# Two layers of sliding-window attention and an MLP on one core: the order of attention turns and dense matmuls decided by a program-side clock, score maxima over 320 columns instead of 384, and staging of MLP weights in value buffers

## The chip, the core and the metric

The kernel runs on one core of a Trainium2 chip. The metric is the time of one execution on the device in microseconds (us); the runs shown of the kernel before have a median of 1614.45 us. Five engines work side by side, each with its own in-order queue: TensorE (PE, with its weight loads as PEld), VectorE (DVE), ScalarE (ACT), GpSimd (POOL) and SyncE (SP, which here only issues DMAs; ACT issues some too). Matmuls write to PSUM; the other engines move results from there to SBUF.

## What is computed

The input is 2048 rows of 640 values. The same pair of layers is applied twice: `x = x + attention(layernorm(x))`, then `x = x + mlp(layernorm(x))`.

```python
def _A_ref(x, wqkv, wo):                      # 32 heads of 20 values, window 256
    q, k, v = ...                             # x @ wqkv, cut into heads
    scores = jnp.einsum("bhqd,bhkd->bhqk", q, k) * (Dh ** -0.5)
    mask = (idx[:, None] - idx[None, :] >= 0) & (idx[:, None] - idx[None, :] < W)
    p = _softmax(jnp.where(mask[None, None], scores, -1e9), axis=-1)
    return heads_joined(p @ v) @ wo
def _B_ref(x, w1, b1, w2, b2):                # 640 -> 1536 -> 640
    h = x @ w1 + b1
    return jnp.where(h > 0, h, 0) ** 2 @ w2 + b2
```

## The kernel before, in words

**Tiling.** The 2048 rows are cut into 8 groups of 256 rows, and with the two layer pairs there are 16 units, numbered u = 0 to 15. Every fp32 operand of a dense matmul is split into a high and a low fp16 part, and three products (high-high, high-low, low-high) are summed; `mm3` (line 261) issues them in steps of about 500 ns. Dense work of a unit: the projections to queries and keys (`stage_qk`, QK below), to values (`stage_v`, V), the output projection (`stage_o`, O), and the two MLP matmuls (`stage_f`, F1 and F2). A dense accumulator is one of two PSUM banks of the pool "mm"; `mm_tile` takes the next free one. The attention output of a pass (`pv`) uses the same pool.

**Attention turns.** The 32 heads of a unit are worked off in 8 quads of four heads. A quad has three turns on PE. The max turn (`max_quad`, MX below, matmuls of lines 570 and 579) computes the scores of four head-and-row blocks into the six PSUM banks `bb`, and eight DVE instructions (line 592) add the mask and take the row maximum. The maxima of two quads are transposed (line 605) and written as extra rows of the queries by DMA. The exp turn (`exp_quad`, EX, lines 647 and 655) computes the transposed scores, with the maxima already subtracted, into the same six banks; six ACT instructions (line 669) take the exponential into `pt`, and POOL cuts the window's edges out (lines 684, 688). The value turn (`pv_quad`, PV, line 718) multiplies by the values. MX runs three quads ahead of EX (`LEAD`). Since MX and EX share the banks `bb`, an MX cannot start before ACT has read the last EX out, and an EX not before DVE has reduced the last MX.

From u = 2 on (`quarters`), MX and EX of a unit that is not the first of a layer cut each matmul into 64-row, 64-column tiles of the array, so that four run side by side and only the 320 of 384 columns that a 64-row half can see are computed. DVE still reads 384 columns. In MX the fourth block does not fit behind the others and is laid across the three banks, 128 columns in each.

**The order of the work** is made by the program itself when it is built. `now[0]` is a running estimate of PE's time, `clk` of the other engines', and `post` puts an instruction of another engine into a list that `pump` empties in order of priority when the estimate allows. `need` moves the estimate forward until a job's estimated end; PE's instruction stream is then written down with whatever comes next, so on the chip PE waits there if the estimate was too early. `flow` orders unit 0. For u = 1 to 15 `together` takes dense steps from a generator and puts in the attention turns when a share of the unit's dense cost is used up (`done < cost * share * part / total`), without asking whether the turn's inputs have come. Dense work that lies beside unit u is V and QK of u+1, O and the MLP of u-1. In u = 14 and 15 there is less of it, and `CARRY`, `KEEP` and `MID` move some from one to the next.

**Places that the change touches.** `load_o` (line 762) fetches a unit's attention output `od` from DRAM and normalizes it: per quarter a reciprocal (line 794), a product (797), a high part on ACT (801) and a low part (804). `stage_o` begins, for u = 0 alone, with `spin(40)`: 40 matmuls of a constant identity (line 275, 80 instructions in the trace, since fp32 takes two passes each), whose result nobody reads. `load_w2` brings the twelve row blocks of the second MLP weight through three thirds of the key buffer `kt2`, which has to be set to a constant (`set_row`) before keys of unit 2 come into it.

## Time and profile before

| | |
|---|---|
| median of 3 runs | 1614.45 us (1614.18 to 1614.67) |
| the profiled execution's own time | 1611.7 us |
| its span, first to last instruction | 1609.9 us |
| busy share: PE, PEld, DVE, ACT, POOL | 98%, 73%, 65%, 46%, 38% |
| granted TensorE clock, mean | 1.00 |

The span is cut below into the stretches between the last PV of one unit and the last PV of the next. "Idle" of PE in a stretch is its length minus PE's busy time. In rows of a timeline the first number is the start in us from the span's start, the second the duration of the merged group; a bracket at the end has the idle time of that engine just ahead of it and what ended it. Since matmuls are pipelined and a matmul's recorded end lies some 0.1 to 0.2 us behind the start of the next, PE times are taken from start to start where possible.

### The profile page before, as it was taken

To read this page: it belongs to the slowest core of one execution; us is meant where nothing else is said; L and a number is where in the kernel's file an instruction comes from. 1 tells how busy PE (TensorE), PEld (TensorE's weight loads), DVE (VectorE), ACT (ScalarE), POOL (GpSimd) and SP (SyncE) were. 2 spreads that over 40 slices of the span, in tenths; PEclk is the share of its full clock that TensorE was granted. 3 is DMA by queue.
4 is the path that set the end of the run, shared out by engine and by line. 5 is a ranking of instruction groups with operands and counts; after the bars stand their busy time and mean duration, and the time that the engine had idled before them with its cause. 6 is when DMAs were issued, how large, how long until landed. Compare 5 with 4: busy or idle time off the path is not lost.

```text
span 1609.9 us, 51896 instructions
## 1 busy us (share of the span) xinstructions
PE 1573.4 (98%) x21222; PEld 1178.3 (73%) x21222; DVE 1044.4 (65%) x3250; ACT 734.3 (46%) x1593; POOL 610.9 (38%) x1288
## 2 busy tenths in 40 slices
PE   8998999999999999999999999999999999998999
PEld 7676767777777777777777777777777777775667
DVE  8786865666757657665556766567675666757441
ACT  4554535344453444545343453534545444453522
POOL 1224434235353443535223352533534334353512
PEclk9999999999999999999999999999999999999999
DMA  9763243352434424343352534334343352431020
GB/s 270 206 169 103 60 121 80 99 127 50 120 84 111 97 67 119 74 121 80 95 133 54 122 80 124 81 95 111 66 115 86 107 109 52 111 73 55 27 65 18
DMA packets 234246, 158.56 MB, mean 98 GB/s; under 512 B 82200, under 2 KB 217752, under 8 KB 234008
## 3 DMA queue, kind: packets, MB, share of 16 engines
q1 hardware_dynamic: 227640, 145.74, 37.2%
q10 hardware_dynamic: 6368, 9.50, 2.0%
q8 instruction: 167, 2.74, 0.8%
q14 instruction: 71, 0.58, 0.1%
HBM read 84.68 MB, written 52.95 MB: 85 GB/s over the span
## 4 chain that ended last, share of the span: by engine, by line
PE 90%; DVE 4%; ACT 3%; issue 1%; DMA 1%; POOL 1%; SPq 0%; DVEq 0%; POOLq 0%; ACTq 0%
PE acc L261 67%; PE pv L718 10%; PE bb L647 4%; PE bb L570 4%; DVE bb L592 2%; ACT pt L669 1%; PE spin L275 1%; PE tr L605 1%; PE bb L655 1%; PE bb L579 1%; DMA od<-o 0%; ACT r L889 0%; DVE mx L592 0%; POOL pt L688 0%; DVE mT L610 0%
## 5 line engine op out<-in xcount | busy, mean ns | idle before, releaser
L592 DVE CUSTOM_DVE_ANT_0 bb<-bb,maskb 128x384 f32<-128x384 f32 (+2 forms) x1024 | 510.6, 566 | 101.0 <-PE bb L570 76.1
L669 ACT ACTIVATE pt<-bb 128x512 f32<-128x512 f32 (+1 forms) x736 | 375.8, 601 | 231.2 <-PE bb L647 199.5
L684 POOL TENSOR_SCALAR_AFFINE_SELECT pt<-pt 128x256 f32<-128x256 f32 x448 | 196.9, 445 | 556.2 <-ACT pt L669 534.3
L261 PE MATMUL acc<-y,w_s 128*128 128x256 f16 x2880 | 330.4, 273 | 4.5 <-DVE y L311 1.5
L261 PE MATMUL acc<-w_s,hh 128*128 128x320 f16 x2304 | 326.2, 299 | 0.0
L261 PEld LDWEIGHTS <-w_s 128*128 128x128 f16 x2880 | 277.4, 98 | 57.2 <-issue 23.5
L261 PEld LDWEIGHTS <-hh 128*128 128x128 f16 x2304 | 221.6, 98 | 96.9 <-issue 12.5
L261 PEld LDWEIGHTS <-wq_s 128*128 128x128 f16 x2400 | 230.6, 98 | 45.7 <-issue 15.2
L261 PE MATMUL acc<-yT,wq_s 128*128 128x256 f16 x2250 | 258.9, 273 | 3.6 <-ACT ot L730 1.6
L688 POOL TENSOR_SCALAR_AFFINE_SELECT pt<-pt 128x256 f32<-128x256 f32 x512 | 218.9, 450 | 94.0 <-ACT pt L669 93.1
L899 DVE TENSOR_TENSOR hh<-r,hh 128x256 f16<-128x256 f32 x192 | 92.6, 505 | 201.3 <-ACT hh L896 195.0
L718 PE MATMUL pv<-pt,vt 128*32 128x128 f32 (+1 forms) x3840 | 186.7, 329 | 2.7 <-DVE x L828 1.7
L893 POOL TENSOR_TENSOR r<-r 128x256 f32<-128x256 f32 x192 | 113.5, 612 | 179.0 <-ACT r L889 177.6
L730 ACT COPY ot<-pv 128x256 f32<-128x256 f32 x128 | 47.6, 372 | 276.6 <-PE pv L718 276.5
L592 DVE DVE_READ_ACCUMULATOR2_ANT mx<- 128x1 f32 x1024 | 144.4, 141 | 0.0
L261 PE MATMUL acc<-wo_s,od 128*128 128x320 f16 x960 | 138.7, 300 | 2.1 <-ACT od L801 1.3
L261 PE MATMUL acc<-wq_s,yT 128*128 128x320 f16 x900 | 132.2, 299 | 3.6 <-DVE y L311 1.9
L718 PEld LDWEIGHTS pv<-pt,vt 128*32 128x32 f32 x3840 | 103.5, 109 | 44.0 <-POOL pt L688 5.7
L889 ACT ACTIVATE r<-acc,b1s 128x256 f32<-128x256 f32 x192 | 80.5, 471 | 98.6 <-PE acc L261 95.8
L261 PEld LDWEIGHTS <-od 128*128 128x128 f16 x960 | 91.4, 98 | 44.7 <-issue 6.0
L261 PEld LDWEIGHTS <-yT 128*128 128x128 f16 x900 | 86.6, 98 | 41.1 <-issue 10.5
L298 POOL TENSOR_TENSOR bmv<-bmv,neghalf 128x1 f32<-128x1 f32 x64 | 43.8, 691 | 138.7 <-DVE bmv L292 137.9
(86 smaller groups left out, 1229.0 us busy)
## 6 DMA issues: line engine op xcount, KB each, us to landing
qt<-qk SPq DMA_DIRECT2D x30, 480.0 KB
kt<-qk SPq DMA_DIRECT2D x30, 480.0 KB
qk<-qd SPq DMA_DIRECT2D x17, 640.0 KB
o<-ot SPq DMA_DIRECT2D x256, 42.0 KB
od<-o SPq DMA_DIRECT2D x14, 640.0 KB
qk<-yl SPq DMA_DIRECT2D x13, 640.0 KB
qk<-qd SPq DMA_DIRECT2D x17, 320.0 KB
xt<-in_A_x_dram SPq DMA_DIRECT2D x16, 320.0 KB
```

Of the source, the lines that this page charges most:

```text
L261: nc.tensor.matmul(acc, lhs(a, c), rhs(b, c), start=(k == 0), stop=(k == 3 * nk - 1))
L570: nc.tensor.matmul(to, qt[r, p, i * P + 64 * h:i * P + 64 * (h + 1)], kt[r, p, a:b], start=True, stop=True, tile_position=(64 * e, 64 * h))
L592: nc.vector.tensor_tensor_reduce(out=v, in0=v, in1=mask, scale=1.0, scalar=-3.0e38, op0=ALU.add, op1=ALU.max, accum_out=accum),
L647: nc.tensor.matmul(bb[e][rows, k, o + a:o + b], kt[r, 2 * qd + j, ko + 64 * h:ko + 64 * (h + 1)], qt[r, 2 * qd + j, q0 * P + a:q0 * P + b] ...
L669: nc.scalar.activation(box["pt"][:, :o], bb[e][:, k, :o], AF.Exp, scale=SCALE / (QS * QS))
L684: nc.gpsimd.affine_select(out=m, in_=m, pattern=[[0, 2], [-1, P]], compare_op=ALU.is_gt, fill=0.0, base=0, channel_multiplier=1)
L688: nc.gpsimd.affine_select(out=m, in_=m, pattern=[[0, 2], [1, P]], compare_op=ALU.is_ge, fill=0.0, base=0, channel_multiplier=-1)
L718: nc.tensor.matmul(pv[32 * jj:32 * (jj + 1), q0 * P:(q0 + qn) * P], vf[:, c:c + 32], pj[:, j, :], start=(k == 0), stop=(k == len(steps) - ...
L730: nc.scalar.copy(ot[:, qd % 2], pv)
L889: nc.scalar.activation(box["r"], acc[:, f, :], AF.Relu, bias=b1s[:, f0 + f:f0 + f + 1], scale=1.0 / (YS * WS))
L893: nc.gpsimd.tensor_tensor(box["r"], box["r"], box["r"], op=ALU.mult)
L899: nc.vector.tensor_sub(hh[:, 1, f, :], box["r"], hh[:, 0, f, :])
```

## The change

1. **MX in packed blocks.** For units that are not the first of a layer each of the four blocks takes 320 columns, one behind the other, over bank borders (0, 320, 640, 960), and a DVE instruction covers 320 columns with a mask `maskq` that is shifted by 64 columns for the upper 64 rows. A piece that would cross a bank border is cut there, so a turn has 38 matmuls instead of 36. For the first unit of a layer the blocks are unbroken (8 matmuls instead of 10), and the mask is `maskw`. Masks are made with one more select and two copies on POOL at the start.
2. **`quarters` holds for u = 1 too**, except its first EX.
3. **Dense work and turns by the program's clock.** Dense generators yield a `Want` (the jobs whose end they need, and whether they need a free accumulator bank) ahead of each place where they would wait. A `Stream` stops there while the estimate says that it isn't due. In `together`, a turn is put in when its share of dense work is done and its own inputs have come by the estimate; if the stream is stopped and the turn's inputs are there, the turn goes first; if neither can go, the estimate moves to the first that can.
4. **No `spin(40)`** ahead of `stage_o(0)`.
5. **`load_w2` has five places** instead of three: two value buffers (`vt4`, `vt5`) and the thirds of `kt2`. The value buffers' constant columns (`set_sums`) are written when their last weight block has gone, and V of unit 2 waits for that. In `load_o` the work of u = 0 has priority 1 instead of 2.

```diff
+    def when(w):
+        if any(j.end is None for j in w.jobs):
+            return None
+        t = max([0.0] + [j.end for j in w.jobs])
+        if w.bank and len(banks2) > 1:
+            free = [max(j.end for j in b) + LAT for b in banks2 if b and all(j.end is not None for j in b)]
+            if not free:
+                return None
+            t = max(t, min(free))
+        return t
...
+        def go(self):
+            while not self.over:
+                if self.want is not None:
+                    t = when(self.want)
+                    if t is None or t > now[0]:
+                        return None
+                    self.want = None
+                c = next(self.gen, "over")
...
-        for c in range(FC):
+        used_by = {}
+        for c, place in enumerate((3, 4, 0, 1, 2, 3, 4, 0, 1, 2, 0, 1)):
...
-            st = krow[2][:, D * (c % 3):D * (c % 3 + 1)]
+            st = vts[1 + place][1][:, :D] if place > 2 else krow[2][:, D * place:D * (place + 1)]
...
-        return u % NG != 0 and u > 1
+        return u % NG != 0
...
+        if quarters(u):
+            flat = [b.rearrange("p a n -> p (a n)") for b in bb]
+            pieces = []
+            for w in range(4):
+                j, i = divmod(w, 2)
+                p, at = 2 * qd + j, 5 * Q * w
+                cuts = sorted({0, 5 * Q, *(z - at for z in (512, 1024) if 0 < z - at < 5 * Q)})
+                for o0, o1 in zip(cuts, cuts[1:]):
                     for h in range(2):
...
+                    reduce(e, w, flat[e][:, 5 * Q * w:5 * Q * (w + 1)], maskq, 5 * Q)
...
+        whole = not quarters(u) or n == NQ
...
-            if u == 0 and i == 0:
-                spin(40)
+            yield Want(*js[2 * i:2 * i + 2])
             need(*js[2 * i:2 * i + 2])
...
+        def work(part, w):
+            nonlocal done
+            while True:
+                t = when(w) if w else None
+                ready = t is not None and t <= now[0]
+                if done >= cost * share * part / total and (ready or not w):
+                    return
+                c = s.go()
+                if c is not None:
+                    done += c
+                elif ready or (s.over and not w):
+                    return
+                else:
+                    wait_any(*([w] if w else []), *([s.want] if s.want else []))
...
-            while done < cost * share * part / total:
-                c = next(dense, None)
-                if c is None:
-                    break
-                step(c)
-                done += c
```

**What moves on the engines.** Between unit 2 and unit 13 PE's dense steps and turns stand in the same order as before; only the pieces within an MX differ. Three places are different and matter below.

PE around O of unit 0 (`spin` is the constant identity, `od` the attention output, `pv` a PV turn; a `bb<-qt,kt` row is of an EX and a `bb<-kt,qt` row of an MX). Before:

```order
L655 MATMUL bb_126<-qt,kt_78 128x256
L275 MATMUL spin<-ident 128x128 x40
L261 LDWEIGHTS od
L261 MATMUL acc<-wo_s,od 128x320
...
L579 LDWEIGHTS qt
```

With the change:

```order
L736 MATMUL bb_130<-qt,kt_86 128x256
L327 LDWEIGHTS wq_s
L327 MATMUL acc<-yT,wq_s 128x256
...
L649 MATMUL bb_130<-kt_86,qt 64x192
L799 MATMUL pv<-pt,vt_89 32x256 x4
L799 MATMUL pv<-pt,vt_88 32x128 x4
L799 MATMUL pv<-pt,vt_91 32x128 x4
L799 MATMUL pv<-pt,vt_90 32x256 x4
L327 LDWEIGHTS od
L327 MATMUL acc<-wo_s,od 128x320
```

Ten QK matmuls, one MX and one PV now stand between the first EX of unit 1 and O, where the constants stood; O's thirty matmuls of its first two accumulators come behind them.

ACT at the start of unit 2 (`qd` is an evicted QK accumulator, `ot` an evicted PV, and line 801, then 882, the high part of the first quarter of O's operand). Before:

```order
L669 ACTIVATE pt<-bb_126 128x512
L435 ACTIVATE qd<-acc 128x2x256
L801 CAST od<-od 128x5x64
L730 COPY ot<-pv 128x256
L435 ACTIVATE qd<-acc 128x2x256
L435 ACTIVATE qd<-acc 128x256
```

With the change:

```order
L750 ACTIVATE pt<-bb_130 128x512
L506 ACTIVATE qd<-acc 128x2x256
L811 COPY ot<-pv 128x256
L506 ACTIVATE qd<-acc 128x2x256
L506 ACTIVATE qd<-acc 128x256
L882 CAST od<-od 128x5x64
```

The CAST has gone from ahead of three evictions that free PSUM banks to behind them.

PE in unit 15, around the second pair of O's accumulators (named by their numbers: before, 25940 and 26022 are the second pair; with the change 26337 is the first of it). Before:

```order
L261 MATMUL acc_25900<-wo_s_103,od_25539 128x320
L261 LDWEIGHTS od_25539
L261 MATMUL acc_25940<-wo_s_103,od_25539 128x320
...
L570 MATMUL bb0_125<-kt2_79,qt_23909 64x128
...
L718 MATMUL pv_25985<-pt_25895,vt5_95 32x256
...
L261 MATMUL acc_26022<-wo_s_103,od_25539 128x320
```

With the change:

```order
L327 MATMUL acc_26270<-wo_s_107,od_25949 128x320
L728 LDWEIGHTS qt_24298
L728 MATMUL bb0_129<-qt_24298,kt2_87 64x192
...
L327 MATMUL acc_26337<-wo_s_107,od_25949 128x320
...
L649 MATMUL bb0_129<-kt2_87,qt_24298 64x256
```

Before, four matmuls of 25940 stood ahead of an MX; now a whole EX stands between the first pair of O's accumulators and the second.

More of the change, by code (lines that the diff above doesn't have):

```diff
@@ L17 @@
 P = 128
+Q = P // 2
 S = 2048
@@ L641, in exp_quad @@
                 for j in range(2):
-                    for h in range(2 if quarters(u) else 0):
+                    for h in range(0 if whole else 2):
                         a, b = (0, w - 64 * (1 - h)) if kb < 2 else (64 * h, w)
@@ L944, in run @@
     def run(*gs):
-        for c in chain(*gs):
-            step(c)
+        s = Stream(chain(*gs))
+        while not s.over:
+            if s.go() is None and not s.over:
+                wait_any(s.want)
     SHARE = 0.55
@@ L1005, in together @@
                 late.clear()
+        work(part, None)
         if whole:
-            run(dense)
+            while not s.over:
+                if s.go() is None and not s.over:
+                    wait_any(s.want)
     QKC, VC, OC, FCST, LNC, CARRY, KEEP, MID = 16.4e3, 8.2e3, 8.2e3, 39.2e3, 1.2e3, 15e3, 20e3, 8e3
```

184 lines of the change are left out of this document (121 added, 63 removed).

## The prediction

> **What bounds the kernel now.** I read the page first, then busy time by stretch, then the waits of PE in the stretches where it is idle.
>
> ```profile
> span 1609.9 us, 51896 instructions
> PE 1573.4 (98%) x21222; PEld 1178.3 (73%) x21222; DVE 1044.4 (65%) x3250; ACT 734.3 (46%) x1593; POOL 610.9 (38%) x1288
> ```
>
> PE is busy 1573.4 of 1609.9 us, so it is idle for 36.5 us, and no other engine comes near it. What can be won is PE's idle time and whatever PE does in vain. The busy time by stretch (length, then PE, PEld, DVE, ACT and POOL busy, clock, DMA share, GB/s) says where the idle time lies; the stretches are unit 0, 1, 2, 3, then 14, 15 and the end.
>
> ```profile
> 0.00:105.60 105.60, 95.66 (x939) 72.82 (x939) 84.13 (x284) 55.16 (x111) 19.41 (x46) 1.00 0.80 218
> 105.60:204.80 99.20, 94.93 (x1139) 70.49 (x1135) 74.19 (x215) 49.02 (x105) 41.96 (x84) 1.00 0.38 98
> 204.80:304.30 99.50, 96.55 (x1394) 72.22 (x1390) 64.08 (x199) 45.14 (x98) 38.77 (x84) 1.00 0.40 98
> 304.30:401.50 97.20, 97.06 (x1402) 72.89 (x1398) 64.46 (x199) 45.37 (x98) 39.51 (x84) 1.00 0.39 95
> 1364.40:1452.40 88.00, 84.84 (x1299) 63.99 (x1296) 57.60 (x182) 43.90 (x96) 39.07 (x82) 1.00 0.35 87
> 1452.40:1534.50 82.10, 73.13 (x1066) 50.35 (x1063) 45.84 (x144) 37.76 (x84) 36.48 (x80) 1.00 0.13 40
> 1534.50:1610.00 75.50, 70.14 (x556) 54.12 (x553) 23.21 (x52) 15.13 (x37) 13.31 (x20) 1.00 0.14 44
> ```
>
> Idle per stretch is 9.9, 4.3, 3.0, 0.1, 3.2, 9.0 and 5.4 us, together 34.9 of the 36.5. Units 3 to 13 leave nothing. So the change is priced at its two ends: units 0 to 2, and units 14 and 15.
>
> **Unit 1: the constants go.** PE around O of unit 0:
>
> ```profile
> 109.52 1.19 PE L655 MATMUL bb<-qt,kt 62*128 62x256 f16 x16
> 110.64 9.20 PE L275 MATMUL spin<-ident 128*128 128x128 f32 x80
> 119.67 4.24 PE L261 MATMUL acc<-wo_s,od 128*128 128x320 f16 x30
> 123.84 0.84 PE L579 MATMUL bb<-kt,qt 60*128 60x128 f16 x18
> 126.35 1.51 PE L718 MATMUL pv<-pt,vt 128*32 128x256 f32 x32 [1.67 <-DVE x L828]
> 127.79 3.30 PE L261 MATMUL acc<-wo_s,od 128*128 128x320 f16 x23
> 136.07 0.84 PE L579 MATMUL bb<-kt,qt 60*128 60x128 f16 x18
> 136.83 1.51 PE L718 MATMUL pv<-pt,vt 128*32 128x256 f32 x32
> 141.73 1.79 PE L261 MATMUL acc<-wq_s,yT 128*128 128x320 f16 x12 [1.37 <-DVE y L311]
> 146.29 2.20 PE L261 MATMUL acc<-wq_s,yT 128*128 128x320 f16 x15 [0.52 <-DVE y L311]
> ```
>
> From the EX at 109.52 to the O rows behind the PV, at 127.79, pass 18.27 us. In them are 80 constant matmuls, 119.67 - 110.64 = 9.03 us, that compute nothing, and a PV that waits 1.67 us. That time isn't simply free: O needs its operand `od`, and DVE has it ready in this order:
>
> ```profile
> 113.60 0.96 DVE L794 RECIPROCAL rs<-rs 128x64 f32<-128x64 f32 x2
> 115.49 0.89 DVE L797 TENSOR_TENSOR od<-od,rs 128x320 f32<-128x320 f32 x2 [0.93 <-DMA od<-o]
> 116.76 0.82 DVE L804 TENSOR_TENSOR od<-od 128x320 f16<-128x320 f32 x2
> ```
>
> The load lands at 115.49, and the second low part, with which O may start, ends at 117.58. With the change ten QK matmuls (0.11 us each, by the row at 219.31 below; 1.1 us) come behind the EX, so the EX starts at about 108.4. The MX must wait for the six exponentials, then PV follows, then O. DVE's order is also another one: from the load's landing it does one product, two reciprocals, a low part, two products, a reciprocal and then the second low part, by the rows above 2 x 0.45 + 0.45 + 3 x 0.48 + 2 x 0.41 = 3.6 us. So `od` is ready at 119.1, or about 118 if the load lands 1.1 us earlier, as the PV ahead of it does. O's thirty matmuls (4.17 us) then end at 122.2 to 123.3, with MX and PV already done. Against 127.79 that is 4.5 to 5.6 us; I take **5.0**. If the load were to land 1 us later it would be 3.6; if it were there at once, the six exponentials, MX (0.7) and PV (1.4) would still hold O. The last four exponentials of that EX are this row:
>
> ```profile
> 111.67 2.08 ACT L669 ACTIVATE pt<-bb 128x512 f32<-128x512 f32 x4
> ```
>
> They end at 113.75, 4.2 us behind the EX's start, so O could not begin before 108.4 + 4.2 + 2.1 = 114.7, which would give 8.9. These are the ends.
>
> What follows in unit 1: MX 136.07 to 136.83 takes 0.76 us with 18 whole matmuls. In the tiled form it takes 0.68, by these rows of unit 2:
>
> ```profile
> 214.33 0.76 PE L570 MATMUL bb<-kt,qt 60*64 60x128 f16 x36
> 215.01 1.51 PE L718 MATMUL pv<-pt,vt 128*32 128x256 f32 x32
> 219.31 1.80 PE L261 MATMUL acc<-yT,wq_s 128*128 128x256 f16 x15 [1.59 <-ACT ot L730]
> 222.20 1.25 PE L261 MATMUL acc<-wq_s,yT 128*128 128x320 f16 x8 [1.10 <-DVE qd L438]
> ```
>
> Eight MX and seven EX become tiled, 15 x 0.08 = **1.2 us**. The waits of 1.37 and 0.52 us behind the transposes of the MLP's input are for an accumulator bank; behind the first of them now stands an EX (0.7 us) that needs none: **0.7** (0 to 1.9).
>
> **Unit 2: an operand that is late no longer blocks evictions.** The two waits in the last rows, 2.7 us, come from one load:
>
> ```profile
> 218.00 0.49 DVE L797 TENSOR_TENSOR od<-od,rs 128x320 f32<-128x320 f32 x1 [1.33 <-DMA od<-o]
> 218.53 0.46 ACT L801 CAST od<-od 128x320 f16<-128x320 f32 x1 [5.63 <-DVE od L797]
> ```
>
> ACT stood 5.63 us at the CAST of `od`, with the evictions of PV and QK queued behind it, and PE waited for those banks. In the changed order the CAST stands behind these evictions on ACT, and DVE does its MX reductions ahead of the product. Both waits should go: **2.7**; if the product is late for the low parts on DVE still, 1.1 of it stays.
>
> **Units 3 to 13: nothing.** PE's order is the same, and an MX has 38 pieces instead of 36. An EX with 32 pieces has the recorded length of an MX with 36:
>
> ```profile
> 1518.82 0.75 PE L647 MATMUL bb<-qt,kt 62*64 62x192 f16 x32
> ```
>
> That is 0.75 against 0.76 us for the same 1280 columns on each of the four tiles, so it is columns and not pieces that count, and I take 0. In proportion to pieces it would be 0.68 x 2/36 = 0.04 us a turn, 4 us in the 112 turns; columns are unchanged, so a gain is excluded. DVE's reductions get shorter:
>
> ```profile
> L592 DVE CUSTOM_DVE_ANT_0 bb<-bb,maskb 128x384 f32<-128x384 f32 x896 | 469.3, 591 | 87.7 <-PE bb L570 76.1 <-PE bb L579 9.1 <-ACT pt L669 1.8
> L592 DVE CUSTOM_DVE_ANT_0 bb<-bb,maskb 128x256 f32<-128x256 f32 x64 | 27.2, 463 | 0.0
> ```
>
> 128 columns are worth 591 - 463 = 128 ns, so 64 are worth 64 ns, 0.51 us over the eight of a turn, 57 us in all 112 turns. In these units it lies beside a PE that is idle for 0.1 us a stretch, and is worth nothing. That a block now spans a bank border shows in no row; DVE reading it slower by as much as a whole turn's 0.5 us would only undo this gain.
>
> **Units 14 and 15.** PE's waits from 1364.4 to 1534.5 (total, times, longest):
>
> ```profile
> PE bb L570 <- ACT pt L669: 3.4, 8, 1.0
> PE bb L647 <- DVE mx L592: 3.4, 9, 1.1
> PE acc L261 <- ACT od L801: 1.3, 1, 1.3
> PE acc L261 <- DVE y L311: 0.9, 1, 0.9
> PE acc L261 <- DVE od L804: 0.8, 1, 0.8
> ```
>
> With little dense work between the turns, MX waits for ACT to empty the banks and EX for DVE. The EX waits: nine, averaging 0.38 us, each turn's worth up to 0.51 less; all but the longest should go, 2.4. The two waits for `od` (2.1) should go, since an EX now stands ahead of the second half of O. Of the MX waits (3.4) and those behind the transposes (0.9, and some smaller ones) I give about half, 2.5, to turns that are put in when the estimate has their banks free; in units 14 and 15 seven of the thirteen distances from an EX to the MX behind it hold more PE work than before, three the same and three less. In all **7 us** (2 to 12, the last being all of the idle 12.2).
>
> **Parts at nothing.** The extra mask work on POOL falls into the first 6 us, where POOL is idle for 3.4 us ahead of line 298:
>
> ```profile
> 5.85 0.55 POOL L298 TENSOR_TENSOR bmv<-bmv,neghalf 128x1 f32<-128x1 f32 x1 [3.44 <-DVE bmv L292]
> ```
>
> One select and two copies, each at most as long as the first two selects by their smaller size, need about 1.5; without that cover the first layernorm would move by as much. The w2 blocks are as many as before, converted by the same instructions and loaded by as many DMAs from ACT's queue; five instead of three are converted ahead of O of unit 0, in a stretch where DVE is busy for 84.1 of 105.6 us, and V of unit 2 now waits for two of them, behind O, where the cover is the rest of unit 1. SP's and POOL's queues get no other instruction.
>
> **Sum.** 5.0 + 1.2 + 0.7 + 2.7 + 7.0 = 16.6 us. The profiled execution took 1611.7 us, 1.8 more than its span, so it should come to 1595.1; the median of the runs, 2.75 above that execution, to **1597.9**.
>
> **Rivals.**
>
> *The array goes cold.* In the new order PE has nothing between the end of PV (108.4 + 4.2 + 0.7 + 1.4 = 114.7) and O at 118 to 119.1: 3.3 to 4.4 us without a matmul. The constants stood exactly there. The trace shows what a rested array does: the first 24 constants of the program took 5.5 us, 0.229 each, against 9.03/80 = 0.113 ahead of O.
>
> ```profile
> L275 PE MATMUL spin<-ident 128*128 128x128 f32 x24 | 5.5, 428 | 1.4 <-POOL ident masks.py:199 1.4
> ```
>
> If that comes back, as many matmuls of O run at half speed: 24 x 0.116 = 2.8 us, giving 1600.7. The granted clock in the rows is 1.00 in every stretch and so doesn't show this state at the start. The Trainium skill, page "TensorE: Matmul & The Clock Gate", section "Part 1: The HAM clock gate", speaks against this part of the change: after an idle window of some 3.4 us, which runs free of the program, the array falls to half its clock, and about as long a busy one brings it back. By that rule a wait as long as this one would sometimes contain a whole window and mostly not; at the program's start the trace agrees. Chance 0.2.
>
> *The tail's waits only move.* The program's estimate, not the chip, says when banks are free; three of the thirteen EX-to-MX distances shrink, one to 2.8 us of PE work (an EX and fifteen matmuls of O, 0.68 + 15 x 0.139) where six exponentials take over 4. If what DVE gives is lost there, the 7 becomes 0: 1604.9. For it: the waits for ACT are as large as those for DVE. Against it: the shrunken ones lie beside O, where ACT evicts nothing else. Chance 0.13.
>
> *Slower: the weight loads of the extra pieces come to light.* A piece of 64 columns streams faster than its weights are loaded (recorded length 107 ns), and the new order has three such pieces in a row on the two tiles of the lower rows, where the old one had no three:
>
> ```profile
> L570 PEld LDWEIGHTS <-qt 60*64 60x64 f16 x3744 | 60.0, 107 | 29.1 <-issue 29.0
> ```
>
> If each of the two extra loads showed in full, a turn would be 0.21 longer, 24 us in 112 turns: 1597.9 + 24 = 1621.9. It decides from 16.6/112 = 0.15 us a turn. Against it: 32 and 36 pieces take the same time today. Chance 0.05.
>
> *The load is there early and the tail gives all:* 5.0 becomes 8.9 and 7 becomes 12: 1589.0. Chance 0.07.
>
> *The change doesn't do what it says:* between units 3 and 13 it doesn't, since PE's order is the same there; that is in the forecast.
>
> **How the numbers follow.** The forecast, 1597.9, has the remaining 0.55. The range leaves out the slower rival and the outermost parts of the others: from 1589.0 (all of the early load and the tail) to 1606.0 (tail lost, with 1 us of the pieces). About 0.2% (3.2 us) is what a measurement of this kernel can tell from no change. Faster by more than that, below 1611.2, are the forecast, the cold array, the moved waits and the early load but for a few per cent where several meet: 0.91; slower, above 1617.7, is the rival with the weight loads: 0.05; same: 0.04.
>
> **What would show it.** No constants behind the first EX of unit 1, and PE idle for 3 to 5 us ahead of O; matmuls of O spaced 139 ns (twice that if cold). The waits at 219.31 and 222.20 gone. Stretches of units 3 to 13 at 97.2 us still, and MX to PV 0.68. Reductions of 320 columns near 527 ns. PE idle in units 14 and 15 at about 5 us instead of 12.2. It would be wrong if units 3 to 13 change in length, if O starts later than before, or if the EX-to-MX waits grow.

## The result, and the profile after

The changed kernel took **1593.83 us** (median of 4 runs, 1593.23 to 1598.94) beside 1614.32 us of the kernel before (4 runs, 1613.78 to 1614.67). The ratio is 0.9879, 95% interval 0.9866 to 0.9893. The forecast was 1597.9 with a range of 1589.0 to 1606.0.

The profiled execution is the slowest of the four, 1598.94 us. A second profile of the same kernel, taken for the experiment `a_again` below (1595.61 us), stands beside it, since the two differ in what matters. Below is the length of each stretch, taken on PE from the matmul behind the last PV of one unit to that of the next (before: 1611.7 us).

| stretch | before | forecast | first profile | second profile |
|---|---|---|---|---|
| units 0 to 2 | 302.92 | -9.6 | 297.40 (-5.5) | 295.15 (-7.8) |
| units 3 to 13 | 1060.09 | 0 | 1062.99 (+2.9) | 1062.83 (+2.7) |
| units 14 and 15 | 170.08 | -7.0 | 159.92 (-10.2) | 159.03 (-11.1) |
| end | 72.14 | 0 | 72.17 | 72.16 |
| all | 1605.23 | -16.6 | 1592.48 (-12.8) | 1589.17 (-16.1) |

From one profiled execution to the other 12.8 or 16.1 us were gained, and 20.5 between the medians: the profile of before was 2.6 us quicker than its median, the first of after 5.1 us slower than its own.

The first lines of the page after the change, and the row of the shortened reductions:

```profile
span 1597.2 us, 52634 instructions
PE 1564.5 (98%) x21590; PEld 1171.1 (73%) x21590; DVE 981.5 (61%) x3251; ACT 735.1 (46%) x1593; POOL 611.3 (38%) x1291
```

```profile
L629 DVE CUSTOM_DVE_ANT_0 bb<-bb,maskq 128x320 f32<-128x320 f32 x896 | 409.0, 522 | 94.9 <-PE bb L649 79.1 <-ACT pt L750 7.3 <-ACT r L974 5.8
```

A reduction takes 522 instead of 591 ns, as forecast (527), and DVE is busy for 63 us less. PE's busy time fell by 8.9 us: 9.03 of constants went. Its idle time fell by only 3.8 us (32.7 instead of 36.5): units 14 and 15 gave 8.8, but unit 1 has 2.3 more than before (6.6 instead of 4.3, from new waits) and units 3 to 13 together 2.8 more. Part of the busy time is now matmuls at half clock, which take longer. Busy time by stretch of the same profile (length, then PE, PEld, DVE, ACT and POOL busy, the granted clock, DMA share, GB/s), for units 1, 2, 3, 14, 15 and the end:

```profile
105.60:200.30 94.70, 88.10 (x1284) 63.45 (x1284) 68.96 (x222) 48.10 (x104) 42.84 (x84) 0.98 0.40 98
200.30:298.80 98.50, 96.23 (x1410) 72.13 (x1406) 59.66 (x199) 45.39 (x98) 39.13 (x84) 1.00 0.42 98
298.80:396.20 97.40, 97.07 (x1418) 72.92 (x1414) 60.10 (x199) 45.40 (x98) 39.11 (x84) 1.00 0.41 95
1361.80:1446.40 84.60, 84.46 (x1323) 63.91 (x1320) 53.33 (x186) 43.84 (x96) 38.56 (x82) 1.00 0.39 90
1446.40:1521.70 75.30, 72.03 (x1082) 51.31 (x1079) 41.63 (x142) 38.99 (x86) 37.94 (x82) 0.98 0.16 48
1521.70:1597.20 75.50, 70.21 (x542) 53.48 (x538) 23.27 (x52) 14.21 (x35) 12.59 (x19) 0.98 0.13 40
```

Two things are to be seen. PE is idle in units 14 and 15 for 0.14 + 3.27 = 3.4 us instead of 12.2. And the clock is 0.98 in three stretches that had 1.00 before. Where the clock fell first shows PE's timeline around O of unit 0 (start, duration; in brackets the idle time ahead and what ended it):

```profile
109.49 0.83 PE L736 MATMUL bb<-qt,kt 62*128 62x256 f16 x16
110.26 1.27 PE L327 MATMUL acc<-yT,wq_s 128*128 128x256 f16 x10
113.46 0.27 PE L649 MATMUL bb<-kt,qt 60*64 60x256 f16 x1 [1.94 <-ACT pt L750]
113.95 0.75 PE L649 MATMUL bb<-kt,qt 60*64 60x256 f16 x37 [0.22 <-ACT pt L750]
114.64 1.87 PE L799 MATMUL pv<-pt,vt 128*32 128x256 f32 x32
118.79 0.45 PE L327 MATMUL acc<-wo_s,od 128*128 128x320 f16 x2 [2.29 <-ACT od L882]
119.51 5.65 PE L327 MATMUL acc<-wo_s,od 128*128 128x320 f16 x28 [0.28 <-DVE od L885]
```

The constants are gone; MX and PV stand in their place. MX waits 1.94 us for the six exponentials, and O behind PV waits another 2.29 us for `od`. Then 28 matmuls of O take 5.65 us, where thirty took 4.24. The same stretch of the second profile, cut along the pieces of 3.41 us in which the trace records the clock (PE's busy time is the second number, the clock the third from the right):

```profile
109.28:112.69 3.41, 1.67 (x24) 1.18 (x19) 3.41 (x6) 2.79 (x6) 2.19 (x3) 1.00 0.85 193
112.69:116.11 3.42, 2.82 (x70) 1.59 (x69) 2.65 (x6) 0.73 (x3) 2.55 (x6) 1.00 0.86 277
116.11:119.52 3.41, 1.03 (x7) 0.55 (x8) 3.28 (x9) 1.49 (x4) 0.00 (x0) 1.00 1.08 206
119.52:122.93 3.41, 3.41 (x15) 1.91 (x14) 3.41 (x15) 0.46 (x1) 0.00 (x0) 0.50 1.16 206
```

One piece in which PE was busy for 1.03 us is followed by one at half clock; after that the clock is full again. The cost is about half a piece: in run 6 below the same 28 matmuls took 3.98 us at full clock, 1.67 us less.

What is left of PE's waits in units 14 and 15 (total, times, longest), first profile:

```profile
PE pv L799 <- POOL pt L769: 1.2, 1, 1.2
PE tr L391 <- DVE y L378: 1.1, 1, 1.1
PE acc L327 <- DVE od L885: 0.3, 1, 0.3
PE bb L649 <- ACT pt L750: 0.2, 1, 0.2
PE bb L728 <- DVE mx L629: 0.2, 1, 0.2
```

The eight waits of MX for ACT (3.4 us), the nine of EX for DVE (3.4) and those for `od` (2.1) have shrunk to 0.2, 0.2 and 0.3. What is left is above all one wait of PV for POOL and one of the transposes, 2.3 us together.

In unit 2 only one of the two waits went. The wait of 1.59 us for the eviction of PV is no longer there; the one for `qd` is, with 1.39 us in the first profile and 0.56 in the second (before: 1.10). DVE stands still until the load of `rs` lands, so its MX reductions and then `qd` come late:

```profile
211.94 0.55 DVE L875 RECIPROCAL rs<-rs 128x64 f32<-128x64 f32 x1 [2.84 <-DMA rs<-o]
216.23 1.25 PE L327 MATMUL acc<-wq_s,yT 128*128 128x320 f16 x8 [1.39 <-DVE qd L509]
```

### The profile page after: what moved, and what is told of

Same layout as the page of the kernel before. It is cut to its first block, busy times and chain, and to the rows that moved or that the text cites. A ratio compares the mean times of both kernels' runs of the same rounds, so it can differ in the third digit from the quotient of the medians.

```text
span 1597.2 us, 52634 instructions
## 1 busy us (share of the span) xinstructions
PE 1564.5 (98%) x21590; PEld 1171.1 (73%) x21590; DVE 981.5 (61%) x3251; ACT 735.1 (46%) x1593; POOL 611.3 (38%) x1291
## 4 chain that ended last, share of the span: by engine, by line
PE 88%; DVE 4%; DMA 3%; ACT 2%; POOL 1%; issue 1%; SPq 1%; DVEq 0%; POOLq 0%; ACTq 0%
PE acc L327 67%; PE pv L799 10%; PE bb L649 5%; PE bb L728 4%; DVE bb L629 1%; PE tr L685 1%; ACT pt L750 1%; DMA x<-in_A_x_dram 1%; POOL x L930 1%; DVE yl L509 1%; DMA xt<-in_B_b_dram 1%; POOL r L978 1%; ACT yl L506 0%; DMA o<-ot 0%; PE spin L341 0%
## 5 line engine op out<-in xcount | busy, mean ns | idle before, releaser
L629 DVE CUSTOM_DVE_ANT_0 bb<-bb,maskq 128x320 f32<-128x320 f32 x896 | 409.0, 522 | 94.9 <-PE bb L649 79.1
L327 PE MATMUL acc<-wo_s,od 128*128 128x320 f16 x960 | 142.3, 302 | 3.2 <-ACT od L882 2.3
```

The source lines that it names most:

```text
L327: nc.tensor.matmul(acc, lhs(a, c), rhs(b, c), start=(k == 0), stop=(k == 3 * nk - 1))
L629: nc.vector.tensor_tensor_reduce(out=v, in0=v, in1=mask, scale=1.0, scalar=-3.0e38, op0=ALU.add, op1=ALU.max, accum_out=accum[e, w]),
```

## The experiments

The theory to be tested was that of the prediction: the order by the clock gives the gain of units 14 and 15 and of unit 2, the missing constants that of unit 1, and the shorter reductions only the waits of EX. Its rival says that the shorter reductions give the ends' gain. Runs 3 and 5 take a part of the change away, and runs 2 and 4 make one part alone; the others follow up what these showed. Ratios are to runs of the kernel before on the same chip; "stretch" has the meaning of the table above.

**1. The changed kernel again.** No edit.

> The changed kernel once more, nothing edited. The profiled execution of the changed kernel took 1598.94 us, three further runs 1593.23 to 1594.11. Theory: it is one kernel with executions that differ by up to 5 us, and most lie at 1593.5. If this run's profile falls among the faster, its stages tell where the 5 us were: I expect fewer than three stretches at half clock (1.7 us each) and the rest in unit 2 or in the waits for DMAs of units 0 to 2. Rival: 1598.9 is as common as 1593.5; then about half of the runs here lie above 1597.

Measured: 1595.76 us (4 runs, 1593.05 to 1596.61), ratio 0.9888 (0.9871 to 0.9904). That most executions lie at 1593.5 us did not hold: one of these four does, the other three took 1595.6 to 1596.6. The theory on the spread holds in part: two stretches at half clock instead of three (119.5 and 1549.7 us; the first profile has 119.9, 1488.6 and 1553.5), which is why unit 15 took 73.78 instead of 75.38 us. Unit 2 took 97.01 instead of 98.55; 0.83 of that is the wait for `qd`, since the load of `rs` held DVE for 2.00 instead of 2.84 us. Unit 0 gave another 0.6; its work is the same in all profiles of this order, and from PE's first matmul it took from 101.9 to 105.3 us.

**2. Only the constants taken out of the kernel before.**

```diff
-            if u == 0 and i == 0:
-                spin(40)
```

> The kernel before with its 80 constant matmuls taken out and nothing else (they compute nothing). Theory: they cover a wait that is mostly real. od was ready at 117.58 and O started at 119.67 us, so O can start 2.1 us earlier; if the array then falls to half clock for one 3.41 us stretch, 1.7 of it is lost again: 0.4 to 2.1 us gained, 1612.3 to 1614.0. Rival: the constants' 9.03 us are on the path in full (od comes earlier without them, or MX and PV fill the place): 1605.4.

Measured: 1615.23 us (10 runs), ratio 1.0011 (1.0001 to 1.0021): **1.8 us slower, not faster**, though only just outside the noise. PE's timeline says why nothing was gained in unit 1:

```profile
110.03 1.19 PE L655 MATMUL bb<-qt,kt 62*128 62x256 f16 x16
118.00 5.93 PE L261 MATMUL acc<-wo_s,od 128*128 128x320 f16 x30 [6.78 <-ACT od L801]
```

O starts 1.67 us earlier (2.1 were estimated), behind 6.78 us of waiting; then its thirty matmuls take 5.93 instead of 4.24 us, and 1.69 are lost again. Unit 1 as a whole took 99.00 us instead of 99.24. The excess of this profile lies elsewhere: unit 2 took 101.32 us instead of 99.51, behind waits for a load and for `mT` (the transposed row maxima) that the profile of before doesn't have. Whether they belong to the edit is open. In the order of before the constants were worth what they cost.

**3. The order by the clock with the reductions of before.** The code of MX and its masks is that of the kernel before, and tiles are used from unit 2 on.

```diff
-        return u % NG != 0
+        return u % NG != 0 and u > 1
...
-                    reduce(e, w, flat[e][:, 5 * Q * w:5 * Q * (w + 1)], maskq, 5 * Q)
+                    v, mask = bb[e][:, w, o:3 * P], maskb[:, o:]
```

> The changed kernel with the MX of before (384 columns a reduction, and whole matmuls in unit 1), so that the order by the clock and the missing constants stand alone. Theory one, the order gives the gain of units 14 and 15 (3.4 + 6.75 us in the profiles) and DVE's shorter reductions only the EX waits (2.4) and the tiled unit 1 (1.2): 1593.8 + 3.6 = 1597.4. Theory two, the shorter reductions give the tail: 1593.8 + 10 + 1.2 = 1605.

Measured: 1631.69 us (4 runs), ratio 1.0118 (1.0102 to 1.0133): **19 us slower than the kernel before and 36 slower than the change**, outside both theories. Unit 4 took 97.8 and unit 5 99.6 us, units 14 and 15 175.7 instead of 170.1. POOL's timeline in unit 5:

```profile
556.99 1.68 POOL L917 TENSOR_TENSOR x<-x,xt 128x320 f32<-128x320 f32 x2 [2.14 <-DMA xt<-in_B_b_dram]
558.62 1.12 POOL L752 TENSOR_SCALAR_AFFINE_SELECT pt<-pt 128x256 f32<-128x256 f32 x3
```

Two additions of the MLP's bias stand ahead of the selects that PV needs. They wait 2.14 us for the bias's load, and the selects wait behind them on POOL:

```profile
562.11 1.71 PE L786 MATMUL pv<-pt,vt 128*32 128x128 f32 x22 [1.34 <-POOL pt L752]
```

How late that load is differs from unit to unit; PV lost 0.6 to 2.5 us in ten of the eleven middle units. The clock did not fall there. It fell in units 14 and 15, where five pieces are at half clock. So the place that the planner chose, not the 64 ns of a reduction, seemed to be the cause, which run 8 tests.

**4. The reductions alone.** The kernel before with the new MX; its constants and order as they were (the reverse of the edit of run 3).

> The kernel before with the new MX (320 columns a reduction, the four pieces of a score block side by side, tiled in unit 1), its order of dense work and its constants as they were. Theory one (the order gives the tail): 2.4 + 1.2 gained, 1614.4 - 3.6 = 1610.8. Theory two (the shorter reductions give it): 10 + 1.2 gained, 1603.2. In both the middle stretches grow by 0.02 us a unit at most, by the 3.4 ns a turn that two more pieces cost; if they grow by 0.2 a unit as in the changed kernel, the 0.2 comes from the pieces or reductions and not from the order.

Measured: 1610.35 us (10 runs), ratio 0.9978 (0.9969 to 0.9988): 3.5 us faster, where theory one had 3.6, but not from the terms that it named. Units 14 and 15 took 166.15 us, 3.9 less than before (2.4 expected). Unit 1, which was to gain 1.2, took 104.11 instead of 99.24: PV waits 3.34 us for DVE there, and the clock falls once. Unit 0 took 3.5 less, so the two together 1.3 more. That the sum came to 3.5 is luck. Two more things were not expected. The middle units took 97.38 us, as in the changed kernel, so the 0.2 us of a unit come with the reductions. And unit 2 took 96.29 instead of 99.51: its two waits went without any clock in the order. ACT's timeline there:

```profile
217.53 0.37 ACT L745 COPY ot<-pv 128x256 f32<-128x256 f32 x1 [3.72 <-PE pv L733]
218.67 0.60 ACT L443 ACTIVATE qd<-acc 128x512 f16<-128x512 f32 x1 [0.77 <-PE acc L269]
220.31 0.38 ACT L443 ACTIVATE qd<-acc 128x256 f16<-128x256 f32 x1 [1.04 <-PE acc L269]
220.84 0.46 ACT L816 CAST od<-od 128x320 f16<-128x320 f32 x1
```

The CAST that held up the evictions for 5.63 us now stands behind them, because the planner, told of shorter reductions, orders the other engines' work differently.

**5. All but the order by the clock.** The changed kernel with turns put in by share of dense work done.

```diff
-            work(part, Want(*wants, bank=kind == "v"))
...
+            while done < cost * share * part / total:
+                c = next(dense, None)
+                if c is None:
+                    break
+                if isinstance(c, Want):
+                    continue
+                step(c)
+                done += c
```

> The changed kernel with turns put in by share of dense work done, as before (the waits on estimated times left out of the order); the shorter reductions, the missing constants and the w2 blocks in value buffers stay. The new MX alone gave units 14 and 15 3.9 of the 10.15 us. Theory one, the rest of the tail's gain (6.3 us) is the order by the clock, and unit 1's gain is the missing constants, which stay missing: 1595 + 6.3 = about 1601.5. Theory two, without the order by the clock the missing constants are worth nothing either (taking them out of the kernel before cost 1.8 us): about the 1610.4 of the new MX alone, or 2 more.

Measured: 1611.71 us (10 runs), ratio 0.9986 (0.9974 to 0.9998). Theory two holds. Without the order by the clock the rest of the change is worth 2 us. Units 14 and 15 took 166.1 us as in run 4, so the order gives the other 7.1 of the 11.1. In unit 1:

```profile
116.00 5.14 PE L327 MATMUL acc<-wo_s,od 128*128 128x320 f16 x23 [5.44 <-ACT od L882]
121.07 0.76 PE L649 MATMUL bb<-kt,qt 60*64 60x256 f16 x38
124.97 1.51 PE L799 MATMUL pv<-pt,vt 128*32 128x256 f32 x32 [3.14 <-DVE x L910]
```

O stands ahead of MX and PV again and waits 5.44 us; MX and PV, which could have filled that time, come behind it, and the half clock lasts two pieces (112.8 to 119.6 us).

**6. Constants in the wait ahead of O.**

```diff
             need(*js[2 * i:2 * i + 2])
+            if u == 0 and i == 0:
+                spin(10)
```

> The changed kernel with 20 constant matmuls (0.113 us each, 2.26 us; they compute nothing) put back between PV and O of unit 0, where PE waits 2.29 us for od and the clock then falls to half for 3.41 us. Theory: the wait is what lets the clock fall, so the record at half speed near 119.5 us goes, O takes 4.2 instead of 5.6 us, and the time falls by 1.5 to 1.7 us, to about 1594.1 beside an unedited 1595.8. Rival: the clock falls anyhow (unit 1 has other waits: 1.94 ahead of MX), or O starts later by what the constants overhang: no change or up to 0.5 us slower.

Measured: 1594.61 us (5 runs, 1591.47 to 1597.84), ratio 0.9878 (0.9862 to 0.9894); no difference from the changed kernel can be told. O ran at full clock (28 matmuls in 3.98 us), as the theory says, but in this execution the clock fell one wait earlier, as the rival says:

```profile
108.43:111.84 3.41, 1.32 (x11) 0.90 (x10) 3.41 (x5) 3.34 (x7) 2.80 (x4) 1.00 0.75 222
111.84:115.25 3.41, 3.33 (x65) 2.36 (x68) 2.12 (x7) 0.03 (x1) 1.94 (x5) 0.50 0.92 275
```

The wait of 1.94 us ahead of MX lay whole in one piece here; in the second profile of the change (rows above, 109.28 to 112.69, PE busy 1.67) the border cut it, and the clock stayed.

**7. The chains of `od` one behind the other on DVE.**

```diff
-            pr = 2 if u else 1
+            pr = 2 + 0.1 * i if u else 1
```

> The changed kernel with the four chains of od ranked one behind the other on DVE (chain i gets priority 2 + 0.1 i in place of 2), PE's order as it is. In units 3 to 13 the second low part of od ends 0.39 us behind O's start in place of 0.38 ahead of it, because the reciprocals of chains 2 and 3 now run ahead of the products, and fifteen matmuls of O take 2.316 instead of 2.131 us. Theory: this wait is the 0.2 us by which each middle unit grew, so they return to 97.2 and the time falls by 11 x 0.185 = 2.0 us, to 1593.7 beside an unedited 1595.8. Rival: ACT's cast of od, behind V's eviction and an exponential, is late whatever DVE does: 97.38 stays.

Measured: 1594.64 us (4 runs), ratio 0.9875 (0.9861 to 0.9888), not to be told from the changed kernel, and the middle units stayed at 97.38. The edit didn't reach its aim, so neither theory was tried: DVE's order around O came out as without it, since the second chain's product isn't ready yet when the third's reciprocal is. Run 11 edits the chains otherwise.

**8. One number of the planner.** Run 3's kernel, told that a reduction of 384 columns takes as long as one of 320; the chip still reads 384.

```diff
-                bbjobs.append(post("D", 113 + 1.047 * (3 * P - o), lambda v=v, mask=mask, accum=accum:
+                bbjobs.append(post("D", 113 + 1.047 * (min(3 * P - o, 320) if quarters(u) else 3 * P - o), lambda v=v, mask=mask, accum=accum:
```

> The kernel with the order by the clock and 384-column reductions (1631.7 us), with one number of the planner changed: it is told that a 384-column reduction takes as long as one of 320 (448 instead of 515 ns). The chip still runs 384 columns. Theory: what cost that kernel 36 us is where the planner's slower clock puts work, not the 64 ns of each reduction (in each middle unit POOL got two additions that wait for a load, ahead of the selects of an EX, and PV waited 0.4 to 1.5 us for them, with the clock at half speed behind the longer ones). Then the middle units return to about 97.2 and the time to 1597 to 1603. Rival: the real length of the reductions is what does not fit into this order: 1625 or more.

Measured: 1605.23 us (4 runs), ratio 0.9944 (0.9931 to 0.9958). **One number, changed to a value that is wrong for this kernel, takes back 26.5 of the 36 us**, and the time lies 2 us above the theory's span, far from the rival's. Unit 4 fell from 97.8 to 97.6 us, unit 5 from 99.6 to 97.6, unit 2 from 99.3 to 96.6, and units 14 and 15 from 175.7 to 162.8 us, with one piece at half clock instead of five. PV's turns, whose excess made the middle units long in run 3, have the length of before again in units 2 to 13. What the remaining 10 us over the changed kernel are was not taken apart. (The expectation's half clock behind PV's waits isn't in the trace of run 3: its middle units have 1.00.) On POOL the bias's additions stand behind the selects again:

```profile
556.48 1.49 POOL L756 TENSOR_SCALAR_AFFINE_SELECT pt<-pt 128x256 f32<-128x256 f32 x3
557.94 3.32 POOL L917 TENSOR_TENSOR x<-x,xt 128x320 f32<-128x320 f32 x4
```

**9. All constants back in the new order.** As run 6, with `spin(40)`.

> The changed kernel with all 80 constant matmuls of before (9.03 us, they compute nothing) put back ahead of O of unit 0; its order stays, so MX and PV stand ahead of them. Theory one (taking the constants out pays because the order by the clock has put MX and PV into the wait that they covered): they now overhang the 2.29 us wait by 6.7 us, less 1.7 for the stretch at half clock that goes, so 5.0 us slower than the changed kernel: 1600 beside 1595. Theory two (unit 1's gain comes from the order alone and the constants lie beside a wait that is there anyhow): within 1 us of the changed kernel.

Measured: 1598.3 us (4 runs), ratio 0.9907 (0.9892 to 0.9922). Theory one holds in its place: unit 1 took 99.69 us instead of 94.56, **5.1 us more**. The clock still fell once in unit 1, behind the wait ahead of MX (113.9 us), but no longer ahead of O:

```profile
113.35 2.32 PE L799 MATMUL pv<-pt,vt 128*32 128x256 f32 x32
115.60 10.00 PE L341 MATMUL spin<-ident 128*128 128x128 f32 x80
125.44 4.24 PE L327 MATMUL acc<-wo_s,od 128*128 128x320 f16 x30
```

By the ratios (0.9879 and 0.9888 for the changed kernel) the whole is 3.1 to 4.5 us slower.

**10. The w2 blocks as before.** `load_w2` with three places, `rowset[2]` behind all twelve blocks, the columns of sums set at the start.

```diff
-        for c, place in enumerate((3, 4, 0, 1, 2, 3, 4, 0, 1, 2, 0, 1)):
+        for c in range(FC):
...
-            if u == 2:
-                yield Want(sums[i], bank=False)
...
-            rowset[2] = [post("D", 460, lambda k=k: set_row(2, k), *[w2j[c] for c in (7, 8, 9, 10, 11)], prio=2) for k in range(4)]
+            rowset[2] = [post("D", 460, lambda k=k: set_row(2, k), *w2j.values(), prio=2) for k in range(4)]
```

> The changed kernel with the w2 blocks loaded as before, three at a time through one row buffer, and the value buffers' columns of sums set at the start. Theory: that part was worth nothing in itself, 1594 to 1596. Rival: the five places let the second row buffer be set earlier and so the QK loads of unit 2, which the order by the clock then uses; without them MX of unit 1 or the first MLP waits, 2 to 5 us slower in units 1 and 2 (in its order the first 24 to 36 matmuls of the MLP's second half stand otherwise).

Measured: 1606.01 us (4 runs, 1600.95 to 1607.81), ratio 0.9951 (0.9936 to 0.9966): **10 us slower** than the changed kernel, more than the rival said. Its mechanism is the rival's, two thirds through unit 1:

```profile
173.56 13.21 PE L324 MATMUL acc<-w_s,hh 128*128 128x320 f16 x96
...
188.07 0.65 PE L644 MATMUL bb<-kt,qt 60*64 60x128 f16 x33 [1.04 <-DMA kt<-qk]
...
201.78 0.24 PE L723 MATMUL bb<-qt,kt 62*64 62x192 f16 x1 [1.94 <-DVE mx L624]
...
205.66 1.77 PE L644 MATMUL bb<-kt,qt 60*64 60x256 f16 x38 [2.38 <-ACT pt L745]
```

MX needs keys of unit 2, whose buffer is free only when all blocks are converted. The order by the clock waits for them by putting in 96 dense matmuls at once; these are missing between the unit's last turns, where EX and MX then wait 1.94 and 2.38 us and the clock is at half for two pieces (202.9 to 209.7). The profiled execution is the quickest of the four by 5 us, so what the others lost besides is open.

**11. Constants in three waits, and the third chain of `od` held back.**

```diff
-            j = post("D", 575, ratio, loaded, prio=pr)
-            j = post("D", 409, times, j, prio=pr)
+            j = post("D", 575, ratio, loaded, prod if 1 < u < NU - 2 and i > 1 else None, prio=pr)
+            j = prod = post("D", 409, times, j, prio=pr)
...
+            if u == 0 and i == 0:
+                spin(10)
...
+            if u == NU - 1 and i:
+                spin(5)
...
+            if warm and k == 1:
+                spin(8)
```

> The changed kernel with three short groups of constants in waits that are there anyhow (16 matmuls ahead of the MX that waits 1.94 us in unit 1, 20 ahead of O that waits 2.29, 10 ahead of the second half of the transposes that wait 1.40 at the end; 0.113 us each, they compute nothing), and with the third chain of od made to wait for the second chain's product on DVE in units 3 to 13 (the priorities alone had left DVE's order as it was). Theory: no stretch at half clock is left, 3.4 us; and each middle unit loses its 0.185 us wait, 2.0 us: 1590 beside an unedited 1595. Rival one: the clock falls somewhere else, 1592 to 1593. Rival two: with the third chain later, fifteen matmuls of O move behind an EX, and that costs what the wait was: 97.38 stays in the middle units.

Measured: 1602.57 us (5 runs), ratio 0.9941 (0.9929 to 0.9954), 8 us slower than the changed kernel. The constants did what they were for: the clock was 1.00 throughout, units 0 to 2 took 294.0 and the end 70.8 us. The chains made it worse: each ordinary middle unit took 98.20 us, with eleven waits for the low part of `od`, 0.41 us on average, where it had lost 0.185:

```profile
PE acc L327 <- DVE od L885: 4.5, 11, 0.4
```

That is rival two's place and more than its size.

**12. The three groups of constants alone.** Run 11 without its first two pairs of lines.

> The changed kernel with the three short groups of constants alone (16, 20 and 10 matmuls, in the waits of unit 1 and of the last transposes; they compute nothing), and the chains of od as in the changed kernel. With the chains edited as well, the clock stayed at full speed throughout, units 0 to 2 came to 294.0 instead of 295.15 us and the end to 70.79 instead of 72.16, while the ten ordinary middle units went from 97.38 to 98.20. Theory: the first two gains stay and the loss goes: 1.1 + 1.4 = 2.5 us faster than the changed kernel, ratio to the kernel before about 0.9865 where the changed kernel has 0.9879 and 0.9888. Rival: the wait for x behind the first half of O (2.2 us, new in that run) takes all of unit 1's part: only the end's 1.4 is left.

Measured: 1594.66 us (4 runs, 1594.51 to 1597.58), ratio 0.9882 (0.9865 to 0.9898): not to be told from the changed kernel. The end's 1.4 us are there (70.79 instead of 72.16). In unit 1 the rival took the gain: O's first half ends earlier and PE then waits for the addition to `x`, which was 0.3 us late in the second profile of the change:

```profile
PE tr L685 <- DVE x L912: 1.8, 1, 1.8
```

The clock fell in unit 0 (48.0 us) and in unit 15 in this execution, where the groups don't stand. So no run here beats the changed kernel by more than can be measured.

## Why the prediction came out

**Unit 1, constants, 5.0 us: the size right, the cause half told.** In the new order the constants are worth 5.1 us (run 9). The working named what holds O: `od` at 118 to 119.1 (118.2 and 118.8 measured), MX and PV done by then. But it booked this to the missing constants. Taken out alone they gain nothing (run 2), and with everything except the order by the clock they bring nothing (run 5). The gain is that the order sets MX and PV into the wait; the constants had covered it.

**Unit 1, the smaller terms.** The tiled turns came about as forecast (1.1 us for 1.2): an MX or EX takes 0.69 us from start to start instead of 0.76. Of the waits for an accumulator the first, 1.37 us, went behind the EX, and the second, 0.52, stayed: more than the 0.7 taken.

**The cold array: the rival of chance 0.2 came in.** Both profiles of the changed kernel have a piece at half clock in unit 1, and one or two more: at the end, and in the first profile in unit 15 too. What failed is the step that weighed it. It counted one wait of 3.3 to 4.4 us; there are two, 1.94 and 2.29 us, and a shorter one was enough. The price is 1.7 us each, not 2.8, since the clock returns after one piece and not after 24 matmuls; and the granted clock does show it. (At the program's start it could not: the record of the clock begins 6.8 us into the profile of before, about when the first 24 constants are through.) Taking 1.7 from the forecast's 9.6 for units 0 to 2 leaves 7.9. The second profile has 7.8, but 0.6 of it is unit 0, where the change does nothing; the first has 5.5.

**Unit 2, 2.7 us: half of the mechanism.** The CAST stands behind the evictions, as said, and the wait of 1.59 us that it caused went. The second wait, 1.10 us, did not go. The prediction named what could hold it, a DVE that is late, but looked at the product; it was the reciprocal ahead of the MX reductions, which waits for `rs`. Unit 2 gained 1.0 us in the first profile and 2.5 in the second. Nor is it the order by the clock that moves the CAST: run 4 has the same order on ACT without it, and both waits are gone there. In run 8 the shorter estimate alone takes unit 2 from 99.3 to 96.6 us. The planner's number for the reductions did it.

**Units 3 to 13, nothing: wrong by 2.7 to 2.9 us.** The step that failed is "PE's order is the same", from which it took that nothing changes. DVE's order isn't the same: with shorter reductions a first `od` chain runs earlier, then two reciprocals stand ahead of the second chain's product, and the first fifteen matmuls of O take 2.316 instead of 2.131 us in each unit. Before (unit 4), the second low part ends ahead of O's start:

```profile
420.62 0.49 DVE L804 TENSOR_TENSOR od<-od 128x320 f16<-128x320 f32 x1
421.50 2.20 PE L261 MATMUL acc<-wo_s,od 128*128 128x320 f16 x15
```

With the change it ends behind it:

```profile
413.93 0.94 DVE L875 RECIPROCAL rs<-rs 128x64 f32<-128x64 f32 x2
416.03 0.56 DVE L885 TENSOR_TENSOR od<-od 128x320 f16<-128x320 f32 x1 [0.42 <-ACT od L882]
416.19 2.39 PE L327 MATMUL acc<-wo_s,od 128*128 128x320 f16 x15
```

That the new MX brings these 0.2 us a unit is shown by run 4. The path through `od` is read from the traces: of the two edits that were to take it away, one did not change DVE's order (run 7) and one made the wait longer (run 11). Another 0.7 us is unit 13 alone (98.05 and 98.08 us), which waits 0.8 us for `mT` in both profiles and in runs 6 and 9 does not; why is open. Two more pieces in an MX cost 3 ns a turn (0.688 instead of 0.685 us), so the dear rival, 210 ns a turn, is refuted as the prediction argued.

**Units 14 and 15, 7 us: too small; 10.2 and 11.1 measured.** Reductions alone gave 3.9 (forecast for the EX waits: 2.4), the order the other 7.1 (forecast for `od` and half of the rest: 4.6). The halved term is what was too small: the waits of MX for ACT went nearly all. The rival by which the waits only move didn't come.

**Parts at nothing: in this order the w2 blocks are worth 10 us.** The prediction looked at V of unit 2, which now waits for two blocks, and at cover for the conversions. It didn't ask what the freed key buffer lets start earlier. In the order by the clock that is MX (run 10).

**Parts do not add.** From the kernel before, the reductions give -3.5 us, all the rest with the old reductions +19, both -18 to -20. A forecast term by term was right in its sum because each term was read from the changed kernel's own order, and because +2.8 in the middle and 1.7 for the clock stood against 4 more in units 14 and 15. That these cancelled is luck.

The Trainium skill, page "TensorE: Matmul & The Clock Gate", section "Part 1: The HAM clock gate", has the window (3.4 us, running free of the program), one busy window to come back, and a whole idle window to fall. The traces agree with the first two: the pieces are 3.41 us on one grid in each profile, and each of the 31 falls ahead of the last matmul ended behind the first piece in which PE was busy for at least 87%. They do not agree with the third: here a piece with PE busy for 1.03, 1.32 or 1.41 of 3.41 us was enough.

## What to carry over

Where a program plans its own queues, ask of each changed duration what the planner does with it on every engine, not only what the instruction saves: one estimate, 448 instead of 515 ns, moved 26 us here. A filler that looks like waste is priced by what would run in its place, so try its removal in the old order and the new one. And a wait of two microseconds on PE can cost 1.7 us more through the clock, depending on where it falls.

## What the hardware showed that was not expected

In the fourteen profiles of this study, cut along the clock's grid up to the last matmul, 21 pieces of 3.41 us at full clock had PE busy for less than 42%; all 21 were followed by a piece at half clock. Of 35 pieces between 42% and 60%, ten were, and of 6433 above 60% none. At half clock it stayed behind the seven pieces with PE busy for at most 69%. What decides between 42% and 60% stayed open. A piece of the first profile that held ten transposes, with a wait of 1.13 us between them, is one of the ten:

```profile
1485.20:1488.61 3.41, 2.01 (x23) 1.24 (x26) 3.41 (x15) 1.95 (x5) 0.00 (x0) 1.00 0.39 132
1488.61:1492.03 3.42, 3.42 (x44) 2.41 (x36) 0.53 (x2) 2.44 (x6) 1.61 (x5) 0.50 0.35 111
```

One of the kernel before with as many transposes and nearly the same busy time was not:

```profile
1563.24:1566.66 3.42, 2.02 (x17) 1.64 (x16) 1.47 (x3) 1.43 (x4) 0.00 (x0) 1.00 0.33 114
```

Since the grid doesn't move with the program, the same wait falls into one piece in one execution and over a border in the next. That accounts for 1.6 us of the spread between executions (unit 15: 73.8 or 75.4). Unit 0's 101.9 to 105.3 us isn't explained by it alone.
